# First weighted values in pairs, joined key and score pieces, and a bias from three bf16 terms

## Chip, cores, metric

One core of a Trainium2 chip. The time is the device time of one execution in microseconds (us). Times of whole kernels are from timed executions; points in time and lengths inside a kernel are from the one profiled execution of each, whose span is some 1.7 us shorter than its time. A halved clock is the granted clock of TensorE as the profile records it. Engines are called as in the profile: PE is TensorE, PEld its weight load, DVE is VectorE, ACT is ScalarE, POOL is GpSimd, SP is SyncE.

## The reference

Shapes: q, k, v are 4 x 8 x 768 x 64, `sort_net` is 4 x 8 x 8 x 8, `w_in` 512 x 2048, `w_out` 2048 x 512. All are f32.

```python
P = sort_net                                   # five rounds of row and column normalisation
for _ in range(5):
    P = P - np.max(P, axis=-1, keepdims=True)
    P = np.exp(P)
    P = P / (np.sum(P, axis=-1, keepdims=True) + 1e-09)
    P = P / (np.sum(P, axis=-2, keepdims=True) + 1e-09)
k_sorted = np.einsum('bhij,bhjcd->bhicd', P, k_b)      # blocks of 96 rows, mixed
v_sorted = np.einsum('bhij,bhjcd->bhicd', P, v_b)
scores = scale * np.matmul(q_b, k_sb.transpose(0, 1, 2, 4, 3))   # within a block
attn = softmax(scores)                                  # (written out in the reference)
x = (attn @ v_sb) as rows of 512                        # (3072 rows, heads side by side)
h = x @ w_in
r = np.maximum(h, 0.0)
g = s * (r * r) + b
out = g @ w_out
```

Since `g @ w_out` is s · (r² @ w_out) + b · (column sums of w_out), the kernel computes the second summand once, as a `bias` row that is the same for all rows.

## The kernel before

The 3072 rows go through in eight half-batches t = 0 to 7 of 384 rows. TensorE works through one long fixed order: the first layer `ffn1(t)` (the matmuls `hps`), the second layer `ffn2(t)` (the matmuls `ops`), and, between groups of four `ops`, small pieces of the attention of later half-batches. A `Queue` deals the pieces out, so many to a slot. Abbreviations in the queues: `S2` is two score pieces (`sc`), `P2` is two weighted-value pieces (`pv`), `K` is one key piece (`tk`), `V2` is one value piece (`tv`), `T` is the transposition of `x` by DMA and `q_turn` that of the queries.

The weighted values of one head pair, and the first ones of the kernel:

```python
def p_piece(t, hp, n0=0, nn=HB):
    ...
    for e in range(2):
        for n in range(n0, n0 + nn):
            nc.tensor.matmul(out=pv[e][...], lhsT=atf[:, c0:c0 + m],
                             rhs=VS[b][:, gi, :], start=True, stop=True)
    rec = rtp.tile([BLK, 2, HB], FP, tag="rec", name="rec")
    nc.vector.reciprocal(out=rec[:, :, 0:nn], in_=pvv[:, :, :, D])
    nc.vector.tensor_tensor(out=x[...], in0=pvv[:, :, :, 0:D], in1=rec[...], op=ALU.mult)
...
for hp in range(NHP):                    # the opening
    p_piece(0, hp, 0, 2)
    if hp == 3:
        t_part(0, 0, "s", 0, 2)
    warm_up(2, psa)
t_part(0, 2, "v", 0, 2)
warm_up(2, psa)
```

The column sums, made on GpSimd after a gate that holds them back until VectorE has written the last of half-batch 1, and the bias on TensorE:

```python
nc.gpsimd.tensor_copy(out=gate, in_=X[1][0:1, HB - 1, d_model - 1:d_model])
... # csum = wo_at(0) + wo_at(1), then csum += wo_at(f), f = 2 to 15, all on GpSimd, f32

def bias_piece():
    bps = psa.tile([128, 2, 512], FP, tag="a", name="bps")
    nc.tensor.matmul(out=bps[:, 0], lhsT=onesf, rhs=csum, start=True, stop=True)
    nc.vector.tensor_scalar(out=bias, in0=bps[:, 0], scalar1=b_bc, scalar2=None, op0=ALU.mult)
    ready.append(True)
    flush()                              # the rows that waited for the bias
```

The queue with the bias, and what follows it on GpSimd, where the loads from memory are issued:

```python
qu = Queue([nothing, lambda: q_piece(1, 2, "v")]
           + [lambda c0=c0: k_piece(1, c0, 16, 1, "vsv"[c0 // 32])() for c0 in range(0, BLK, 32)]
           + [seq(lambda: load_q(2), lambda: load_k(*brows(2)), bias_piece), V2[0], S2(2, 0), V2[1], S2(2, 2), V2[2], V2[3],
              P2(2, 0), V2[4], P2(2, 2), V2[5], S2(3, 0),
              seq(T(2), K(2, 0, 16, "s")), P2(3, 0), S2(3, 2), K(2, 32, 16, "s"), P2(3, 2), T(3),
              seq(lambda: q_turn(2), K(2, 64, 16, "s"))], 24)
ffn2(0, qu)
ffn2(1, qu)
ffn1(2)
ffn1(3)
nc.gpsimd.tensor_copy(out=gate2, in_=QT[2][0:1, NHP - 1, S - 1:S])   # waits for q_turn(2)
v_read(2, nc.gpsimd)                     # the weighted-value blocks vs of batch 2
load_k(*brows(3))
```

The softmax here doesn't subtract the row's maximum and nothing guards it: scores larger than these inputs give would overflow.

Of the kernel before, what the change touches and what calls it, by code (L numbers as in the profile page):

```python
# [18 lines left out]
def kernel(  # L19
# [74 lines left out]
    def load_k(rows, prow, n=1):  # L94
        for c0 in range(0, BLK, BLK // n):
            cs = slice(c0, c0 + BLK // n)
            nc.gpsimd.dma_start(out=kb[prow, cs, :], in_=kraw[rows, cs, :])
# [16 lines left out]
    VS = {}  # L114
# [37 lines left out]
    for c0 in range(0, d_ff, FCH):  # L152
# [1 line left out]
        nc.gpsimd.dma_start(  # L154
            out=w, in_=moe_w_in.rearrange("(hp p) f -> p hp f", p=128)[:, :, c0:c0 + FCH])
        wis.append(w)
    onesf = const.tile([128, 128], FP)
    nc.gpsimd.memset(onesf, 1.0)

    load_v(*brows(1))  # L160
    for f0 in range(0, NF, FW):
# [17 lines left out]
    def warm_up(n, pool=psb):  # L179
        wp = pool.tile([128, 256], FP, tag="b" if pool is psb else "a", name="wp")  # L180
        for _ in range(n):
            nc.tensor.matmul(out=wp, lhsT=zt[:, 0:128], rhs=zt, start=True, stop=True)  # L182
# [198 lines left out]
    def p_piece(t, hp, n0=0, nn=HB):  # L381

        b, half = divmod(t, 2)
        at = AT[t, hp]
        if t not in X:
            X[t] = xp.tile([BLK, HB, d_model], BF, tag="x", name="x")
        x = X[t]
        atf = at.rearrange("p e t -> p (e t)")
        if nn < HB:
            p1 = psb.tile([128, 512], FP, tag="b", name="pv")  # L390
            pv = [p1[:, e * nn * VW:(e + 1) * nn * VW] for e in range(2)]
            pvv = p1[0:BLK, 0:2 * nn * VW].rearrange("p (e n w) -> p e n w", e=2, w=VW)
        else:
            p2 = psa.tile([128, 2, 512], FP, tag="a", name="pv")
            pv = [p2[:, 0], p2[:, 1]]
            pvv = p2[0:BLK, :, 0:nn * VW].rearrange("p e (n w) -> p e n w", w=VW)
        for e in range(2):
            for n in range(n0, n0 + nn):
                c0 = (e * HB + n) * BLK
                m = 128 if c0 + 128 <= 2 * TG else BLK  # L400
                gi = e * 32 + hp * NB + half * HB + n
                nc.tensor.matmul(out=pv[e][0:m, (n - n0) * VW:(n - n0 + 1) * VW],  # L402
                                 lhsT=atf[:, c0:c0 + m],
# [3 lines that stand above are left out]
        nc.vector.tensor_tensor(  # L407
            out=x[:, n0:n0 + nn, hp * 128:(hp + 1) * 128].rearrange("p n (e d) -> p e n d", e=2),
            in0=pvv[:, :, :, 0:D],
            in1=rec[:, :, 0:nn].unsqueeze(3).broadcast_to([BLK, 2, nn, D]), op=ALU.mult)  # L410

    def t_piece(t, eng, n0=0, nn=HB):

        x = X[t]
        if t not in XT:
            XT[t] = xtp.tile([128, NHP, TG], BF, tag="xt", name="xt")
        if nn < HB:
            t1 = psb.tile([128, 1024], BF, tag="b", name="tr")
            tr = [t1[:, hp * nn * BLK:(hp + 1) * nn * BLK] for hp in range(NHP)]
            src = t1[:, 0:NHP * nn * BLK]  # L420
            dst = XT[t][:, :, n0 * BLK:(n0 + nn) * BLK]
            src = src.rearrange("p (a t) -> p a t", a=NHP)
        else:
            t2 = psa.tile([128, 2, 1024], BF, tag="a", name="tr")
            tr = [t2[:, hp // 2, (hp % 2) * TG:(hp % 2 + 1) * TG] for hp in range(NHP)]
            src = t2[:, :, 0:2 * TG]
            dst = XT[t].rearrange("p (a b) t -> p a (b t)", b=2)
        for hp in range(NHP):
            for n in range(n0, n0 + nn):
                nc.tensor.transpose(out=tr[hp][:, (n - n0) * BLK:(n - n0 + 1) * BLK],  # L430
                                    in_=x[:, n, hp * 128:(hp + 1) * 128],
                                    identity=ident[0:BLK, 0:BLK])
        evac(dst, src, eng)

    def t_part(t, hp0, eng, n0, nn):

        if t not in XT:
            XT[t] = xtp.tile([128, NHP, TG], BF, tag="xt", name="xt")
        tr = psa.tile([128, 2, 1024], BF, tag="a", name="tr")
        for i in range(2):  # L440
            hp = hp0 + i
            for n in range(n0, n0 + nn):
                nc.tensor.transpose(out=tr[:, 0, (i * nn + n - n0) * BLK:(i * nn + n - n0 + 1) * BLK],
                                    in_=X[t][:, n, hp * 128:(hp + 1) * 128],
                                    identity=ident[0:BLK, 0:BLK])
        evac(XT[t][:, hp0:hp0 + 2, n0 * BLK:(n0 + nn) * BLK],
             tr[:, 0, 0:2 * nn * BLK].rearrange("p (a t) -> p a t", a=2), eng)
# [13 lines left out]
    def nothing():  # L461
        pass

    def ffn1(t, slot=nothing, n0=0, nn=HB):
        if t not in GT:
            GT[t] = gtp.tile([128, NF, TG], BF, tag="gt", name="gt")
        gt = GT[t]
        c0, nt = n0 * BLK, nn * BLK
        for f0 in range(0, NF, 2):
            hps = psa.tile([128, 2, 512], FP, tag="a", name="hps")  # L470
            for f in range(2):
                for hp in range(NHP):
                    nc.tensor.matmul(out=hps[:, f, 0:nt], lhsT=wi_at(hp, f0 + f),  # L473
                                     rhs=xt_at(t, hp, n0, nn),
                                     start=(hp == 0), stop=(hp == NHP - 1))
            rt = rtp.tile([128, 2, TG], BF, tag="rt", name="rt")
            nc.scalar.activation(out=rt[:, :, 0:nt], in_=hps[:, :, 0:nt], func=AF.Relu)  # L477
            nc.vector.tensor_tensor(out=gt[:, f0:f0 + 2, c0:c0 + nt], in0=rt[:, :, 0:nt],  # L478
                                    in1=rt[:, :, 0:nt], op=ALU.mult)
            slot()  # L480
# [59 lines left out]
    def seq(*fs):  # L540
        def run():
            for f in fs:
                f()
        return run

    def S2(t, hp):
        return lambda: (s_piece(t, hp), s_piece(t, hp + 1))
# [9 lines left out]

    def bias_piece():
        bps = psa.tile([128, 2, 512], FP, tag="a", name="bps")
        nc.tensor.matmul(out=bps[:, 0], lhsT=onesf, rhs=csum, start=True, stop=True)  # L560
        nc.vector.tensor_scalar(out=bias, in0=bps[:, 0], scalar1=b_bc, scalar2=None,
                                op0=ALU.mult)
        ready.append(True)
        flush()
# [33 lines left out]
    v_piece0(56, 8, "v")  # L598
    s_piece(0, 2)
    s_piece(0, 3)  # L600
    for hp in range(NHP):
        p_piece(0, hp, 0, 2)
        if hp == 3:
            t_part(0, 0, "s", 0, 2)
        warm_up(2, psa)
    t_part(0, 2, "v", 0, 2)
    warm_up(2, psa)

    load_v(*brows(2))

# [1 line left out]
    def P(t, hp, *r):  # L612
        return lambda: p_piece(t, hp, *r)

    def SC(t, hp):
        return lambda: s_piece(t, hp)

    def V1(i, eng="s"):
        return lambda: v_piece1(i * 8, eng)

    ffn1(0, Queue([P(0, 0, 2, 2), P(0, 1, 2, 2), P(0, 2, 2, 2), P(0, 3, 2, 2),
                   lambda: q_half(1, "s"), lambda: t_piece(0, "v", 2, 2), SC(1, 0), SC(1, 1)], 8), 0, 2)
    ffn1(0, Queue([seq(SC(1, 2), P(1, 0)), V1(0), seq(SC(1, 3), P(1, 1)), V1(1), P(1, 2), P(1, 3),
                   seq(V1(2), V1(3)), lambda: t_piece(1, "v")], 8), 2, 2)
    V1(4)()
    V1(5)()
# [17 lines left out]
    load_v(*brows(3))  # L644
    csums(8, NF)

    def K(b, c0, nc2, eng):
        return lambda: k_piece(b, c0, nc2, 1, eng)()

    V2 = [lambda c0=c0: v_piece2(c0, "s") for c0 in range(0, BLK, 16)]  # L650
    qu = Queue([nothing, lambda: q_piece(1, 2, "v")]
               + [lambda c0=c0: k_piece(1, c0, 16, 1, "vsv"[c0 // 32])() for c0 in range(0, BLK, 32)]
               + [seq(lambda: load_q(2), lambda: load_k(*brows(2)), bias_piece), V2[0], S2(2, 0), V2[1], S2(2, 2), V2[2], V2[3],
                  P2(2, 0), V2[4], P2(2, 2), V2[5], S2(3, 0),
                  seq(T(2), K(2, 0, 16, "s")), P2(3, 0), S2(3, 2), K(2, 32, 16, "s"), P2(3, 2), T(3),
                  seq(lambda: q_turn(2), K(2, 64, 16, "s"))], 24)
    ffn2(0, qu)
    ffn2(1, qu)

# [6 lines left out]
    v_read(3, nc.gpsimd)  # L666
    load_q(3)
    qu = Queue([S2(4, 0), nothing, nothing, P2(4, 0), nothing, S2(4, 2), nothing, nothing,
                P2(4, 2), nothing, T(4), K(3, 0, 16, "v"), S2(5, 0), nothing, K(3, 32, 16, "s"),
                P2(5, 0), nothing, S2(5, 2), nothing, P2(5, 2), K(3, 64, 16, "s"), T(5),  # L670
                lambda: q_turn(3), nothing], 24)
    ffn2(2, qu)
    ffn2(3, qu)
# [39 lines left out]
```

## Time and profile before

| | before |
|---|---|
| time, median of 3 (range) | 233.44 us (233.39 to 233.68) |
| span of the profiled run | 231.6 us |
| PE busy | 224.3 us, 97% of the span |
| DVE, ACT, POOL busy | 50%, 49%, 21% |

The prediction below shows the main lines and reads them. TensorE is the bound: it hardly waits after the opening. One row of the view of what TensorE waits for says how little there is to win by removing waits (columns: engine and tile, what it waited for, us in total, times, longest):

```profile
PE ops L516 <- DVE ot L490: 0.4, 1, 0.4
```

This is the wait after the bias. After the start-up, up to 27 us, the view has only one more of note, 0.3 us for a Relu in the opening.

### The profile page before, as it was taken

The numbers are of one execution on the slowest core, as the hardware profiler recorded it, in microseconds if no ns is written. First come the engines' busy times: TensorE is split into PE (matmuls) and PEld (weight loads), VectorE is DVE, ScalarE is ACT, GpSimd is POOL, SyncE is SP. The second block draws the span as 40 slices with busy tenths as digits, with TensorE's granted clock in tenths as the row PEclk, the third lists the DMA queues.
The fourth block names the chain that finished last, engine by engine and source line by source line (L and its number), as shares of the span: only waits on it lengthen the run. The fifth ranks groups of instructions, "written<-read, shape, count | busy, mean of one in ns | idle before, by whom it ended". The sixth has DMA issues, their size and how long they took to land.

```text
span 231.6 us, 4837 instructions
## 1 busy us (share of the span) xinstructions
PE 224.3 (97%) x2036; PEld 136.8 (59%) x2036; DVE 116.8 (50%) x245; ACT 114.6 (49%) x164; POOL 48.3 (21%) x62
## 2 busy tenths in 40 slices
PE   8879999999999999999999999999999999999994
PEld 6779887765544555566555555665555556554442
DVE  5778566638992645244446653343452634432221
ACT  6168479685158486856630645656222236660000
POOL 7820000399992000007920000000000000000000
PEclk9975699999999999999999999999999999999999
DMA  5999999998799992764999995610115240001212
GB/s 93 142 200 211 226 193 205 231 220 183 106 110 180 273 312 63 161 82 65 130 148 133 183 197 115 93 47 0 46 47 113 93 110 4 3 0 45 80 59 91
DMA packets 46695, 28.90 MB, mean 125 GB/s; under 512 B 35921, under 2 KB 41041, under 8 KB 46161
## 3 DMA queue, kind: packets, MB, share of 16 engines
q0 software_dynamic: 18800, 15.21, 47.8%
q1 hardware_dynamic: 27728, 13.32, 26.6%
q8 instruction: 16, 0.26, 0.5%
q10 hardware_dynamic: 144, 0.07, 0.1%
q14 instruction: 7, 0.05, 0.1%
HBM read 29.63 MB, written 8.65 MB: 165 GB/s over the span
## 4 chain that ended last, share of the span: by engine, by line
PE 82%; DVE 7%; DMA 5%; ACT 3%; issue 1%; POOL 0%; POOLq 0%
PE hps L473 35%; PE ops L516 31%; DMA qr<-in_q_dram 5%; PE pv L402 4%; PE sc L375 3%; DVE gt L478 2%; ACT ks L240 2%; DVE ks L238 2%; PE tv L320 2%; PE ops L501 2%; PE tk L294 1%; PE tv L350 1%; PE wp L182 1%; PE tq L254 1%; PE tv L336 1%
## 5 line engine op out<-in xcount | busy, mean ns | idle before, releaser
L473 PE MATMUL hps<-xt,wi 128*128 128x384 bf16 (+1 forms) x576 | 87.1, 309 | 0.3 <-ACT rt L477 0.3
L516 PE MATMUL ops<-wo,gt 128*128 128x512 bf16 x368 | 86.9, 380 | 0.4 <-DVE ot L490 0.4
L473 PEld LDWEIGHTS <-wi 128*128 128x128 bf16 x576 | 54.1, 98 | 30.6 <-issue 1.3
L477 ACT ACTIVATE rt<-hps 128x768 bf16<-128x768 f32 (+1 forms) x72 | 53.1, 741 | 37.4 <-PE hps L473 37.0
L478 DVE TENSOR_TENSOR gt<-rt 128x768 bf16<-128x768 bf16 (+1 forms) x72 | 41.2, 574 | 50.2 <-ACT rt L477 50.0
L516 PEld LDWEIGHTS <-gt 128*128 128x128 bf16 x368 | 33.6, 98 | 37.2 <-issue 1.0
L378 ACT ACTIVATE at<-sc 96x768 bf16<-96x768 f32 x32 | 24.4, 804 | 27.7 <-PE sc L375 27.7
L490 DVE SCALAR_TENSOR_TENSOR ot<-ops,s_bc,bias 128x512 f32<-128x512 f32 x23 | 17.1, 749 | 41.2 <-PE ops L516 41.2
L240 ACT CAST ks<-tk 64x512 bf16<-64x512 f32 (+1 forms) x32 | 18.6, 582 | 10.5 <-PE tk L294 10.2
L407 DVE TENSOR_TENSOR x<-pv,rec 96x512 bf16<-96x512 f32 (+1 forms) x36 | 22.6, 627 | 1.3
L639 POOL TENSOR_TENSOR csum<-csum,wo 128x512 f32<-128x512 f32 x14 | 17.6, 1254 | 1.0
L402 PEld LDWEIGHTS <-at 96*128 96x128 bf16 (+1 forms) x256 | 12.0, 104 | 3.8
L182 PE MATMUL wp<-zt 128*128 128x256 bf16 x86 | 12.9, 311 | 1.1 <-DVE warm L113 1.1
L238 DVE CAST ks<-tk 64x512 bf16<-64x512 f32 (+1 forms) x20 | 13.0, 651 | 1.1 <-PE tk L294 0.8
L402 PE MATMUL pv<-vs,at 96*128 96x66 bf16 (+1 forms) x256 | 13.0, 199 | 0.1
L240 ACT CAST vn<-tv 128x512 bf16<-128x512 f32 (+1 forms) x12 | 9.4, 799 | 7.2 <-PE tv L350 5.0
L375 PEld LDWEIGHTS <-ks 64*96 64x96 bf16 x256 | 8.6, 128 | 5.8 <-issue 5.1
L406 DVE RECIPROCAL rec<-pv 96x8 f32<-96x8 f32 (+1 forms) x36 | 6.9, 192 | 9.5 <-PE pv L402 9.4
L84 POOL DMA_DIRECT2D qr<-in_q_dram x12 | 10.6, 912 | 4.8 <-DMA kb<-in_k_dram 3.1
L375 PE MATMUL sc<-qt,ks 64*96 64x96 bf16 x256 | 10.9, 219 | 0.1
L182 PEld LDWEIGHTS <-zt 128*128 128x128 bf16 x86 | 9.0, 110 | 2.6 <-DVE warm L113 1.1
L294 PEld LDWEIGHTS <-kb 64*128 64x128 bf16 x192 | 6.7, 99 | 3.9 <-issue 3.4
(73 smaller groups left out, 98.4 us busy)
## 6 DMA issues: line engine op xcount, KB each, us to landing
out_dram<-ot SPq DMA_DIRECT2D x23, 256.0 KB, 2.4
kb<-in_k_dram POOLq DMA_DIRECT2D x4, 768.0 KB, 12.2
vb<-in_v_dram POOLq DMA_DIRECT2D x4, 768.0 KB, 19.0
wi<-in_moe_w_in_dram POOLq DMA_DIRECT2D x2, 1024.0 KB, 19.7
wo<-in_moe_w_out_dram POOLq DMA_DIRECT2D x2, 1024.0 KB, 32.6
qr<-in_q_dram POOLq DMA_DIRECT2D x12, 128.0 KB, 13.5
dv<-vn SPq DMA_DIRECT2D x6, 256.0 KB, 7.5
vs<-dv POOLq DMA_DIRECT2D x4, 384.0 KB, 12.7
```

What stands on the lines that cost most here:

```text
L182: nc.tensor.matmul(out=wp, lhsT=zt[:, 0:128], rhs=zt, start=True, stop=True)
L238: nc.vector.tensor_copy(out=out, in_=in_)
L240: nc.scalar.copy(out=out, in_=in_)
L375: nc.tensor.matmul(out=sc[:, e, n * BLK:(n + 1) * BLK], lhsT=ks[pr, g0 + n, :], rhs=QT[b][pr, hp, q0:q0 + BLK], start=True, stop=True)
L378: nc.scalar.activation(out=at, in_=sc[:, :, 0:TG], func=AF.Exp, scale=scale)
L402: nc.tensor.matmul(out=pv[e][0:m, (n - n0) * VW:(n - n0 + 1) * VW], lhsT=atf[:, c0:c0 + m], rhs=VS[b][:, gi, :], start=True, stop=True)
L407: nc.vector.tensor_tensor(out=x[:, n0:n0 + nn, hp * 128:(hp + 1) * 128].rearrange("p n (e d) -> p e n d", e=2), in0=pvv[:, :, :, 0:D], in1 ...
L473: nc.tensor.matmul(out=hps[:, f, 0:nt], lhsT=wi_at(hp, f0 + f), rhs=xt_at(t, hp, n0, nn), start=(hp == 0), stop=(hp == NHP - 1))
L477: nc.scalar.activation(out=rt[:, :, 0:nt], in_=hps[:, :, 0:nt], func=AF.Relu)
L478: nc.vector.tensor_tensor(out=gt[:, f0:f0 + 2, c0:c0 + nt], in0=rt[:, :, 0:nt], in1=rt[:, :, 0:nt], op=ALU.mult)
L516: nc.tensor.matmul(out=ops, lhsT=gt[:, f, m * 128:(m + 1) * 128], rhs=wo_at(f), start=(f == 0), stop=(f == NF - 1))
L639: nc.gpsimd.tensor_tensor(out=csum, in0=csum, in1=wo_at(f), op=ALU.add)
```

## The change

Its intent is to take time out of TensorE's order in three ways: a quicker opening, fewer switches between full-height and 64-row matmuls (in the trace of before, four `ops` take 0.97 us after 64-row scores and 0.86 after a full-height product), and a bias without f32 matmuls.

Opening: weighted values of two head pairs at once, and a first layer that begins its first two `hps` tiles on the first two head pairs.

```diff
+    def p_pair(t, hp0, n0):             # two head pairs: 8 matmuls, one reciprocal, one multiply
+        ...
+        p2 = psa.tile([128, 4, 256], FP, tag="a", name="pv")
+        ...
-    for hp in range(NHP):
-        p_piece(0, hp, 0, 2)
-        if hp == 3:
-            t_part(0, 0, "s", 0, 2)
-        warm_up(2, psa)
+    warm_up(2)
+    p_pair(0, 0, 0)
+    warm_up(4)
+    p_pair(0, 2, 0)
+    t_part(0, 0, "s", 0, 2)
+    warm_up(3)
     t_part(0, 2, "v", 0, 2)
-    warm_up(2, psa)
...
-    def ffn1(t, slot=nothing, n0=0, nn=HB):
+    def ffn1(t, slot=nothing, n0=0, nn=HB, lead=0):
+        for f0 in range(0, lead, 2):    # lead = 4 in the first call only
+            begun[f0] = psa.tile([128, 2, 512], FP, tag="a", name="hps")
+            products(f0, begun[f0], range(0, NHP // 2))
...
-    ... seq(SC(1, 3), P(1, 1)), V1(1), P(1, 2), P(1, 3), ...
+    ... seq(SC(1, 3), P(1, 1)), P(1, 2), V1(1), P(1, 3), ...
```

Bias: the f32 column sums are split into three bf16 terms on GpSimd, and three bf16 matmuls add them up.

```diff
+    cparts = const.tile([128, 3, d_model], BF)
+    for i in range(3):
+        nc.gpsimd.tensor_copy(out=cparts[:, i], in_=csum)
+        if i < 2:
+            nc.gpsimd.tensor_tensor(out=csum, in0=csum, in1=cparts[:, i], op=ALU.subtract)
...
-        nc.tensor.matmul(out=bps[:, 0], lhsT=onesf, rhs=csum, start=True, stop=True)
+        for i in range(3):
+            nc.tensor.matmul(out=bps[:, 0], lhsT=ones, rhs=cparts[:, i], start=(i == 0),
+                             stop=(i == 2))
```

Joined pieces: key and score pieces share slots, one query copy goes to ScalarE, and `P2(3, 2)` comes one slot later.

```diff
-    qu = Queue([nothing, lambda: q_piece(1, 2, "v")]
-               + [... three key pieces of batch 1, one to a slot ...]
-               + [seq(lambda: load_q(2), lambda: load_k(*brows(2)), bias_piece), V2[0], ..., V2[5], S2(3, 0),
-                  seq(T(2), K(2, 0, 16, "s")), P2(3, 0), S2(3, 2), K(2, 32, 16, "s"), P2(3, 2), T(3),
-                  seq(lambda: q_turn(2), K(2, 64, 16, "s"))], 24)
+    qu = Queue([nothing, seq(lambda: q_piece(1, 2, "s"), K(1, 0, 16, "v")), nothing,
+                seq(K(1, 32, 16, "s"), K(1, 64, 16, "v")), nothing,
+                seq(lambda: load_q(2), lambda: load_k(*brows(2)), bias_piece),
+                V2[0], ..., V2[5],
+                seq(T(2), S2(3, 0), K(2, 0, 16, "v")), nothing, P2(3, 0), nothing,
+                seq(S2(3, 2), K(2, 32, 16, "s")), nothing, P2(3, 2),
+                seq(T(3), lambda: q_turn(2), K(2, 64, 16, "s"))], 24)
... the same for batch 3: S2(5, 0) with K(3, 0), S2(5, 2) with K(3, 32)
```

More of the change, by code (lines that the diff above doesn't have):

```diff
@@ L156 @@
         wis.append(w)
-    onesf = const.tile([128, 128], FP)
-    nc.gpsimd.memset(onesf, 1.0)
+    ones = const.tile([128, 128], BF)
+    nc.gpsimd.memset(ones, 1.0)
     load_v(*brows(1))
@@ L410, in p_piece @@
             in1=rec[:, :, 0:nn].unsqueeze(3).broadcast_to([BLK, 2, nn, D]), op=ALU.mult)
+    def p_pair(t, hp0, n0):
+        b, half = divmod(t, 2)
+        if t not in X:
+            X[t] = xp.tile([BLK, HB, d_model], BF, tag="x", name="x")
+        p2 = psa.tile([128, 4, 256], FP, tag="a", name="pv")
+        for i in range(2):
+            atf = AT[t, hp0 + i].rearrange("p e t -> p (e t)")
+            for e in range(2):
+                for n in range(2):
+                    c0 = (e * HB + n0 + n) * BLK
+                    gi = e * 32 + (hp0 + i) * NB + half * HB + n0 + n
+                    nc.tensor.matmul(out=p2[:, 2 * i + e, n * VW:(n + 1) * VW],
+                                     lhsT=atf[:, c0:c0 + 128], rhs=VS[b][:, gi, :],
+                                     start=True, stop=True)
+        pvv = p2[0:BLK, :, 0:2 * VW].rearrange("p a (n w) -> p a n w", w=VW)
+        rec = rtp.tile([BLK, 4, 2], FP, tag="rec", name="rec2")
+        nc.vector.reciprocal(out=rec, in_=pvv[:, :, :, D])
+        nc.vector.tensor_tensor(
+            out=X[t][:, n0:n0 + 2, hp0 * 128:(hp0 + 2) * 128].rearrange(
+                "p n (a d) -> p a n d", d=D),
+            in0=pvv[:, :, :, 0:D], in1=rec.unsqueeze(3).broadcast_to([BLK, 4, 2, D]),
+            op=ALU.mult)
     def t_piece(t, eng, n0=0, nn=HB):
@@ L468, in ffn1, with products @@
         c0, nt = n0 * BLK, nn * BLK
-        for f0 in range(0, NF, 2):
-            hps = psa.tile([128, 2, 512], FP, tag="a", name="hps")
+        begun = {}
+        def products(f0, hps, part):
             for f in range(2):
-                for hp in range(NHP):
+                for hp in part:
                     nc.tensor.matmul(out=hps[:, f, 0:nt], lhsT=wi_at(hp, f0 + f),
@@ L475, in ffn1 @@
                                      start=(hp == 0), stop=(hp == NHP - 1))
+        for f0 in range(0, lead, 2):
+            begun[f0] = psa.tile([128, 2, 512], FP, tag="a", name="hps")
+            products(f0, begun[f0], range(0, NHP // 2))
+        for f0 in range(0, NF, 2):
+            if f0 in begun:
+                hps = begun[f0]
+                products(f0, hps, range(NHP // 2, NHP))
+            else:
+                hps = psa.tile([128, 2, 512], FP, tag="a", name="hps")
+                products(f0, hps, range(NHP))
             rt = rtp.tile([128, 2, TG], BF, tag="rt", name="rt")
@@ L600 @@
     s_piece(0, 3)
-    for hp in range(NHP):
-        p_piece(0, hp, 0, 2)
-        if hp == 3:
-            t_part(0, 0, "s", 0, 2)
-        warm_up(2, psa)
+    warm_up(2)
[4 more added lines that the diff above has]
+    warm_up(3)
     t_part(0, 2, "v", 0, 2)
-    warm_up(2, psa)
     load_v(*brows(2))
@@ L621 @@
     ffn1(0, Queue([P(0, 0, 2, 2), P(0, 1, 2, 2), P(0, 2, 2, 2), P(0, 3, 2, 2),
-                   lambda: q_half(1, "s"), lambda: t_piece(0, "v", 2, 2), SC(1, 0), SC(1, 1)], 8), 0, 2)
-    ffn1(0, Queue([seq(SC(1, 2), P(1, 0)), V1(0), seq(SC(1, 3), P(1, 1)), V1(1), P(1, 2), P(1, 3),
+                   lambda: q_half(1, "s"), lambda: t_piece(0, "v", 2, 2), SC(1, 0), SC(1, 1)], 8), 0, 2, 4)
+    ffn1(0, Queue([seq(SC(1, 2), P(1, 0)), V1(0), seq(SC(1, 3), P(1, 1)), P(1, 2), V1(1), P(1, 3),
                    seq(V1(2), V1(3)), lambda: t_piece(1, "v")], 8), 2, 2)
@@ L650 @@
     V2 = [lambda c0=c0: v_piece2(c0, "s") for c0 in range(0, BLK, 16)]
-    qu = Queue([nothing, lambda: q_piece(1, 2, "v")]
-               + [lambda c0=c0: k_piece(1, c0, 16, 1, "vsv"[c0 // 32])() for c0 in range(0, BLK, 32)]
-               + [seq(lambda: load_q(2), lambda: load_k(*brows(2)), bias_piece), V2[0], S2(2, 0), V2[1], S2(2, 2), V2[2], V2[3],
-                  P2(2, 0), V2[4], P2(2, 2), V2[5], S2(3, 0),
-                  seq(T(2), K(2, 0, 16, "s")), P2(3, 0), S2(3, 2), K(2, 32, 16, "s"), P2(3, 2), T(3),
-                  seq(lambda: q_turn(2), K(2, 64, 16, "s"))], 24)
+    qu = Queue([nothing, seq(lambda: q_piece(1, 2, "s"), K(1, 0, 16, "v")), nothing,
+                seq(K(1, 32, 16, "s"), K(1, 64, 16, "v")), nothing,
+                seq(lambda: load_q(2), lambda: load_k(*brows(2)), bias_piece),
+                V2[0], S2(2, 0), V2[1], S2(2, 2), V2[2], V2[3], P2(2, 0), V2[4], P2(2, 2), V2[5],
+                seq(T(2), S2(3, 0), K(2, 0, 16, "v")), nothing, P2(3, 0), nothing,
+                seq(S2(3, 2), K(2, 32, 16, "s")), nothing, P2(3, 2),
+                seq(T(3), lambda: q_turn(2), K(2, 64, 16, "s"))], 24)
     ffn2(0, qu)
@@ L668 @@
     qu = Queue([S2(4, 0), nothing, nothing, P2(4, 0), nothing, S2(4, 2), nothing, nothing,
-                P2(4, 2), nothing, T(4), K(3, 0, 16, "v"), S2(5, 0), nothing, K(3, 32, 16, "s"),
-                P2(5, 0), nothing, S2(5, 2), nothing, P2(5, 2), K(3, 64, 16, "s"), T(5),
+                P2(4, 2), nothing, T(4), nothing, seq(S2(5, 0), K(3, 0, 16, "v")), nothing, nothing,
+                P2(5, 0), nothing, seq(S2(5, 2), K(3, 32, 16, "s")), nothing, P2(5, 2),
+                K(3, 64, 16, "s"), T(5),
                 lambda: q_turn(3), nothing], 24)
```

## The prediction

> **What bounds the kernel now.** I read the page first (busy slices, clock row, shares of the chain), then the chain in order of time, then the timeline at the three places that the diff touches, and last the engine that the diff gives new work, GpSimd (POOL).
>
> ```profile
> PE   8879999999999999999999999999999999999994
> PEclk9975699999999999999999999999999999999999
> PE 82%; DVE 7%; DMA 5%; ACT 3%; issue 1%; POOL 0%; POOLq 0%
> ```
>
> After the fifth slice (about 29 us) TensorE is busy in at least 90% of every slice but the last, and at full clock. The clock is low only from about 14 to 28 us. What shortens the kernel is therefore TensorE time taken out; what makes TensorE wait anywhere after 28 us is added to the end. The 7% of the chain on VectorE lie mostly between 54 and 70 us, where TensorE was nevertheless busy and VectorE's backlog ends in one wait of 0.41 us at 70.32.
>
> The opening, from the timeline and from the table of stretches (columns: stretch, length, busy time of PE, PEld, DVE, ACT, POOL, clock, DMA share, GB/s):
>
> ```profile
> 26.90 0.63 PE L182 MATMUL wp<-zt 128*128 128x256 bf16 x2
> 27.14 0.36 DVE L238 COPY xt<-tr 128x384 bf16<-128x384 bf16 x1 [0.43 <-PE tr L443]
> 27.32 1.05 PE L473 MATMUL hps<-xt,wi 128*128 128x192 bf16 x8
> ...
> 27.00:28.00 1.00, 1.00 (x10) 0.86 (x8) 0.36 (x1) 0.00 (x0) 0.00 (x0) 0.62 1.07 221
> ```
>
> The first layer (hps) starts only after the second transposed pair is copied. A mean clock of 0.62 over 27 to 28 us, half before and full after, puts the release at 27.76 (0.5x + 1 - x = 0.62, x = 0.76).
>
> The slots where weighted sums interleave with the second layer, from the chain in order of time (start, length, what):
>
> ```profile
> 80.78 0.43 PE tv L350 x2
> 81.21 0.86 PE ops L516 x4
> 82.08 0.49 PE sc L375 x16
> 82.56 0.97 PE ops L516 x4
> 83.53 0.58 PE tk L294 x16
> ```
>
> The same four ops matmuls take 0.86 after another full-height product but 0.97 after the 64-row scores (sc). The keys (tk) behave alike.
>
> The bias, from the timelines of POOL and of TensorE, and the wait that follows it:
>
> ```profile
> 44.73 1.14 POOL L637 TENSOR_TENSOR csum<-wo 128x512 f32<-128x512 bf16 x1
> 45.95 7.91 POOL L639 TENSOR_TENSOR csum<-csum,wo 128x512 f32<-128x512 f32 x6
> 53.81 0.54 POOL L100 DMA_DIRECT2D vb<-in_v_dram  x1
> 54.37 10.59 POOL L639 TENSOR_TENSOR csum<-csum,wo 128x512 f32<-128x512 f32 x8
> 64.90 5.31 POOL L84 DMA_DIRECT2D qr<-in_q_dram  x6
> 70.15 0.59 POOL L97 DMA_DIRECT2D kb<-in_k_dram  x1
> ```
>
> ```profile
> 66.06 1.03 PE L560 MATMUL bps<-csum,onesf 128*128 128x512 f32 x2
> 66.93 1.03 PE L516 MATMUL ops<-wo,gt 128*128 128x512 bf16 x4
> ...
> 70.32 1.02 PE L516 MATMUL ops<-wo,gt 128*128 128x512 bf16 x4 [0.41 <-DVE ot L490]
> ```
>
> This is the fact on which the prediction turns: POOL ends the column sums at 64.96 and TensorE uses them at 66.06, only 1.1 us later. POOL looks idle on the page (21%), but in this stretch it is full and almost on the critical path.
>
> [...] the trace has 1.14 to 1.36, median 1.26. [...] the drop at 14.12 (clock 0.56 over 14 to 15 us) and the release at 27.76 are 13.64 us apart[...].
>
> **The change part by part.**
>
> *Opening.* Four weighted-value pieces of one head pair become two of two. On VectorE that is 2 x (0.20 + 0.69) = 1.78 us in place of 4 x (0.18 + 0.42) = 2.40 (rows of rec and x, 512 and 256 elements). But the second pair now needs the fourth exponential, which ScalarE ends at 24.83. From there: eight products 0.5, rec and x 0.95, transposes 0.35, so the last transposes end near 27.0. The first-layer matmuls on the first two head pairs need not await the second copy and start at about 27.0, against 27.52 in the chain. The clock is still half until about 27.76, so the 0.5 us hold three matmuls of 160 ns, worth 82 ns each later: gain about 0.3 us.
>
> *Order of the later pieces.* One weighted-value piece is put before a value piece. In before, the two pieces at 41.3 and 42.25 fill the accumulators, and the chain shows 0.57 us (42.42 to 42.99) in which TensorE waits for the Relu. I take 0.35 us of it back.
>
> *Joined pieces.* Two key pieces share a slot once, and score and key pieces share one four times: five joins. A separate 64-row piece costs 0.11 on the way out and, from the starts in the timeline (ops end at 72.47, scores start at 72.57), some 0.1 on the way in, of which part is hidden; I take 0.15 each. One join lies before the bias, four after: 0.15 and 0.60 us.
>
> *One copy moved.* A query copy of 1.75 us goes from VectorE to ScalarE, which was idle for 4.79 us there. This removes the 0.41 us wait after the bias.
>
> *Bias.* On TensorE three bf16 matmuls of 512 columns (0.216 each, from ops: 0.86 for four) replace an f32 matmul in two passes that took 0.87: 0.65, a gain of 0.22 if all is ready. On POOL five operations come after the column sums: three copies to bf16 and two subtractions. Subtractions: 2 x 1.26 = 2.52. A copy of 512 is not in the trace; from POOL's memsets (0.21 for 128 elements, 0.30 for 256)[...], my estimate is 0.65, so 1.95. With the gaps of 0.07 between POOL operations: 4.8 us. The compiled order confirms that the three terms' matmuls wait for one copy each, and that these five stand before the six query loads and the key load.
>
> TensorE would reach the bias 0.3 + 0.35 + 0.15 = 0.8 us earlier, at 65.25. The sums start when the last weighted value of the second half is written, so they shift by 0.65: end 64.3, the third term at 69.1, the third matmul's end at 69.4. Before, the bias ended at 66.93. TensorE is 2.5 us behind there, although it has 0.8 us less to do. All later work waits in TensorE's order, so it counts in full.
>
> Sum on the path: +2.5 at the bias, -0.4 for the wait that goes, -0.6 for the four later joins = +1.5 us.
>
> **Two things that may be added.** The wait is about 4 us (65.25 to 69.4), broken by two short matmuls. [...] And the query and key loads of the third batch leave POOL some 4.2 us later: the key load is issued at about 74.4. It took 12.3 us before, much of it behind the query loads, and landed near 82.5 to 83; the key piece, now one slot earlier, wants it near 84. If it still takes 12.3 us, TensorE waits some 2 us; if the shorter queue lets it land in 7 to 9, nothing. +0.4 on average. The two overlap: a TensorE slowed by its clock waits less for the keys.
>
> **The rivals.** (1) The gains go through: POOL's five operations fit into the slack. Then 0.8 + 0.2 + 0.4 + 0.6 = 2 us less, 231.4. For it: the page's POOL share of 21%, and that whoever made the change can be supposed to have wanted this. Against it: 1.1 us of slack, plus 0.43 for two matmuls, against 4.8 us of work; even copies of 0.3 us make 3.7. (2) The wait is there, the clock falls and the keys are late too: +4.5 to +5.5, 238 to 239. [...] (3) The wait is there but shorter, 2 us, and the other gains cancel it: 233.5 to 234.5. For it: copies might be quicker than I estimate.
>
> **Range and chances.** The sum with the means of the two additions is +2.8, or 236.2; rival 1 and 3 pull it down, and I put the value at 235.6 us. The range is 232.3 to 238.4. Over 2% faster is below 228.8 us: no part can give 4.6 us, chance 0.01. Over 2% slower is above 238.1 us: it needs both additions nearly in full, 0.12. Within 2%: 0.87.
>
> **What would show it.** In the profile after: POOL's row with three copies near 0.65 and two subtractions near 1.26 from about 64.3 to 69.1; TensorE waiting on POOL at the bias matmuls by 3 to 4 us in all; no wait of the ops on ot just after; a clock below 1 in the slice after 69 us[...]; perhaps a wait of the first key piece on its load; the hps starting near 27.0; score and key pieces back to back with one 0.97 after them. The prediction is wrong if POOL's terms are ready within 2 us of the sums, or if TensorE comes to the bias much later than 65 us.

One term of its sum: +0.9 us for a halved clock at the bias (1.3 to 1.7 us with a chance of 0.6), of which length and chance were the author's estimate. With that term the sum came to 1.5 + 0.9 + 0.4 = +2.8 us, and the half clock is in the second rival's 4.5 to 5.5 too. The "1.14 to 1.36, median 1.26" are GpSimd's two-input operations of 512 elements in the trace of before. For a copy of 512, a line through the two memsets gives 0.48 us; the rest up to 0.65 was the author's estimate and not shown.

## The result

The changed kernel took 237.75 us (median of 4 runs, 237.52 to 237.87), the kernel before 233.43 us (median of 4, 233.39 to 233.68). All were fast runs. The ratio is 1.0182, with a 95% interval of 1.0164 to 1.0199: slower by 1.8%, inside the predicted range and 2.15 us above the predicted value. Ratios here and below are the mean time of one kernel's fast runs over that of the other's in the same rounds, so they are not quite the ratio of the medians. Executions over 1.5% slower than the fastest of the same kernel are left out of the means.

The page of the changed kernel, its busy slices, clock row and chain shares:

```profile
PE   8979999999949999999979999999999999999994
PEclk9975899999997999999999999999999999999999
PE 56%; issue 17%; POOL 13%; DVE 5%; DMA 5%; ACT 3%; POOLq 0%
```

Where before had nines there is now a 4 in the 12th slice (65 to 71 us), a clock of 7 in the slice behind it, and a 7 in the 21st (118 to 124 us). POOL, which had 0% of the chain that ended last, has 13%.

The timeline of POOL at the bias (start, length, line, operation):

```profile
64.87 0.61 POOL L687 CAST cparts<-csum 128x512 bf16<-128x512 f32 x1
65.56 1.15 POOL L689 TENSOR_TENSOR csum<-csum,cparts 128x512 f32<-128x512 f32 x1
66.78 0.61 POOL L687 CAST cparts<-csum 128x512 bf16<-128x512 f32 x1
67.46 1.15 POOL L689 TENSOR_TENSOR csum<-csum,cparts 128x512 f32<-128x512 f32 x1
68.68 0.61 POOL L687 CAST cparts<-csum 128x512 bf16<-128x512 f32 x1
...
74.48 0.60 POOL L97 DMA_DIRECT2D kb<-in_k_dram  x1
```

The five operations lie end to end from 64.87 to 69.29: 4.4 us. Only then do the loads follow, so the key load is issued at 74.48 instead of 70.15.

The timeline of TensorE at the same place; the bracket gives the idle time before, and what ended it:

```profile
65.53 0.38 PE L597 MATMUL bps<-cparts,ones 128*128 128x512 bf16 x1
67.44 0.38 PE L597 MATMUL bps<-cparts,ones 128*128 128x512 bf16 x1 [1.53 <-POOL cparts L687]
69.34 0.38 PE L597 MATMUL bps<-cparts,ones 128*128 128x512 bf16 x1 [1.53 <-POOL cparts L687]
69.56 0.68 PE L552 MATMUL ops<-wo,gt 128*128 128x512 bf16 x2
```

TensorE comes to the bias at 65.53, finds the first term just finished, and then twice waits 1.53 us. The `ops` after the bias start at 69.56; before, at 66.93. That is 2.63 us late, although TensorE had arrived 0.53 us earlier.

The table of stretches over the same time (columns: stretch, length, busy of PE, PEld, DVE, ACT, POOL, then the mean granted clock):

```profile
69.00:70.00 1.00, 0.66 (x3) 0.29 (x3) 0.24 (x1) 0.00 (x0) 1.00 (x2) 0.97 0.14 12
70.00:71.00 1.00, 0.78 (x3) 0.41 (x3) 0.96 (x2) 0.00 (x0) 1.00 (x2) 0.50 0.04 3
...
73.00:74.00 1.00, 1.00 (x19) 0.46 (x18) 0.40 (x1) 0.09 (x1) 1.00 (x2) 0.83 1.34 267
```

A mean of 0.97 puts the halving 0.06 us before 70, at 69.94; a mean of 0.83 puts the release 0.34 us after 73, at 73.34. So the clock was half for 3.40 us.

The third place is at 122 us, in the view of the changed kernel's waits:

```profile
PE bps L597 <- POOL cparts L687: 3.1, 2, 1.5
PE pv L402 <- DMA vs<-dv: 1.2, 1, 1.2
```

The first row is the bias again. The second was nowhere in the prediction: weighted values of batch 2 wait for `vs`, their blocks of v. The way to it starts with the transposition of `x` of half-batch 3, whose query transposes come behind it on the same queue and open the gate for the loads of `vs`. From the timelines of SP's queue and of TensorE, before:

```profile
91.74 1.28 SPq L452 DMA_TRANSPOSE xt<-x  x1
...
117.24 0.70 PE L402 MATMUL pv<-vs,at 96*128 96x66 bf16 x16
```

and after:

```profile
97.11 1.49 SPq L476 DMA_TRANSPOSE xt<-x  x1
...
122.07 0.69 PE L402 MATMUL pv<-vs,at 96*128 96x66 bf16 x16 [1.22 <-DMA vs<-dv]
```

Before, TensorE began the first layer of half-batch 2 at 92.38, 0.64 us after that transposition; after, at 95.83, 1.28 us ahead of it. The transposition has slipped by 1.9 us against TensorE. In both kernels the loads of `vs` are issued some 14 us after it (105.82 and 110.95).

How late TensorE is against before, place by place, shows where the time went:

| place | before | after | late by |
|---|---|---|---|
| second layer of half-batch 0 starts | 57.96 | 57.74 | -0.22 |
| bias | 66.06 | 65.53 | -0.53 |
| first `ops` after the bias | 66.93 | 69.56 | 2.63 |
| `ops` after the second score piece | 70.32 | 73.98 | 3.66 |
| first layer of half-batch 2 starts | 92.38 | 95.83 | 3.45 |
| weighted values of half-batch 4 | 117.24 | 122.07 | 4.83 |
| span | 231.6 | 236.0 | 4.4 |

From the third row to the fourth 1.03 us are lost. The half clock took more than that, since TensorE no longer waits for VectorE there: the same code takes 2.73 us from the one place to the other at full clock (69.97 to 72.70 in the filler run below) and 4.42 us here, so about 1.7 us. From the fourth to the fifth the joins give back 0.21, from the fifth to the sixth the new wait makes up 1.22 of 1.38 us, and after it the last two joins bring the lag from 4.83 down to 4.4.

The opening went earlier at its start and not at its end. From the timeline of TensorE after:

```profile
26.84 0.34 PE L467 MATMUL tr<-ident,x 96*128 96x96 bf16 x4 [0.51 <-DVE x L430]
27.02 1.16 PE L498 MATMUL hps<-xt,wi 128*128 128x192 bf16 x12
...
29.70 0.31 PE L402 MATMUL pv<-vs,at 96*128 96x66 bf16 x4 [0.25 <-DVE x L407]
```

The `hps` start at 27.02 as predicted (27.32 before). But since two of them are begun together, the first is complete later in the order, and its Relu starts on ScalarE only 0.19 us earlier (28.21 against 28.40). VectorE's work behind that Relu ends with the multiply `x` at 29.64, and at 29.70 TensorE has waited 0.25 us for it. At the query transposes that follow, it is still 0.19 us ahead (31.41 against 31.60), in a run whose clock happened to be released at 25.56 instead of 27.76.

### The profile page after: what moved, and what is told of

Same layout as the page of the kernel before. It is cut to its first block, busy times and chain, and to the rows that moved or that the text cites. A ratio compares the mean times of both kernels' runs of the same rounds, so it can differ in the third digit from the quotient of the medians.

```text
span 236.0 us, 4818 instructions
## 1 busy us (share of the span) xinstructions
PE 222.7 (94%) x2016; PEld 136.0 (58%) x2036; DVE 118.1 (50%) x244; ACT 113.5 (48%) x161; POOL 52.4 (22%) x67
## 4 chain that ended last, share of the span: by engine, by line
PE 56%; issue 17%; POOL 13%; DVE 5%; DMA 5%; ACT 3%; POOLq 0%
PE ops L552 23%; PE hps L498 21%; POOL csum L677 7%; DMA vs<-dv 4%; PE sc L375 3%; PE pv L402 2%; POOL qr L84 2%; PE tv L320 2%; PE ops L537 1%; ACT ks L240 1%; POOL csum L689 1%; POOL cparts L687 1%; DVE x L407 1%; PE tq L254 1%; DMA sn<-in_sort_net_dram 1%
## 5 line engine op out<-in xcount | busy, mean ns | idle before, releaser
L552 PE MATMUL ops<-wo,gt 128*128 128x512 bf16 x348 | 84.0, 383 | 1.5 <-issue 0.5
L514 DVE TENSOR_TENSOR gt<-rt 128x768 bf16<-128x768 bf16 (+1 forms) x72 | 41.7, 581 | 49.0 <-ACT rt L513 48.8
L552 PEld LDWEIGHTS <-gt 128*128 128x128 bf16 x368 | 34.3, 99 | 39.9 <-issue 3.1
L407 DVE TENSOR_TENSOR x<-pv,rec 96x512 bf16<-96x512 f32 (+1 forms) x32 | 20.9, 654 | 1.2
L240 ACT CAST ks<-tk 64x512 bf16<-64x512 f32 (+1 forms) x28 | 16.3, 582 | 3.6 <-PE tk L294 3.3
L238 DVE CAST ks<-tk 64x512 bf16<-64x512 f32 (+1 forms) x24 | 15.8, 658 | 3.1 <-PE tk L294 2.7
L240 ACT CAST vn<-tv 128x512 bf16<-128x512 f32 (+1 forms) x12 | 9.4, 800 | 10.5 <-PE tv L350 9.8
L182 PE MATMUL wp<-zt 128*128 128x256 bf16 x85 | 12.5, 314 | 1.1 <-DVE warm L113 1.1
L402 PEld LDWEIGHTS <-at 96*128 96x128 bf16 x240 | 10.5, 102 | 4.9 <-issue 1.7
L402 PE MATMUL pv<-vs,at 96*128 96x66 bf16 x240 | 11.3, 195 | 1.5 <-DMA vs<-dv 1.2
L84 POOL DMA_DIRECT2D qr<-in_q_dram x12 | 10.6, 912 | 4.7 <-DMA kb<-in_k_dram 2.9
L406 DVE RECIPROCAL rec<-pv 96x8 f32<-96x8 f32 (+1 forms) x32 | 6.2, 195 | 6.7 <-PE pv L402 6.7
L240 ACT COPY qt<-tq 128x768 bf16<-128x768 bf16 (+1 forms) x6 | 5.9, 1014 | 5.0 <-PE tq L254 3.3
```

Of the source, the lines that this page charges most:

```text
L182: nc.tensor.matmul(out=wp, lhsT=zt[:, 0:128], rhs=zt, start=True, stop=True)
L240: nc.scalar.copy(out=out, in_=in_)
L402: nc.tensor.matmul(out=pv[e][0:m, (n - n0) * VW:(n - n0 + 1) * VW], lhsT=atf[:, c0:c0 + m], rhs=VS[b][:, gi, :], start=True, stop=True)
L407: nc.vector.tensor_tensor(out=x[:, n0:n0 + nn, hp * 128:(hp + 1) * 128].rearrange("p n (e d) -> p e n d", e=2), in0=pvv[:, :, :, 0:D], in1 ...
L514: nc.vector.tensor_tensor(out=gt[:, f0:f0 + 2, c0:c0 + nt], in0=rt[:, :, 0:nt], in1=rt[:, :, 0:nt], op=ALU.mult)
L552: nc.tensor.matmul(out=ops, lhsT=gt[:, f, m * 128:(m + 1) * 128], rhs=wo_at(f), start=(f == 0), stop=(f == NF - 1))
```

## The experiments

Theory: the terms on GpSimd are the loss (2.6 us of lateness and the half clock), the later `P2(3, 2)` causes the wait for `vs`, and opening and joins gain a little. Rival 1: the joins lose by themselves, since they ask for keys sooner. Rival 2: the lost time is half clock, and a busy TensorE would get it back. Three batches ran on three chips; the kernel before had medians of 233.25, 233.36 and 233.24 us there. Every kernel gave correct results. Ratios are against before.

| kernel | time, fast runs (us) | ratio, 95% interval |
|---|---|---|
| changed, bias in f32 | 233.54 to 235.62 (3) | 1.0054, 0.9997 to 1.0112 |
| before, with the three terms | 235.72 to 238.44 (4) | 1.0167, 1.0120 to 1.0214 |
| changed, filler between the terms | 236.38 to 237.66 (4) | 1.0161, 1.0131 to 1.0192 |
| changed, `P2(3, 2)` and `T(3)` as before | 236.59 to 238.32 (4) | 1.0184, 1.0151 to 1.0218 |
| before, with the opening | 233.14 to 233.72 (5) | 1.0003, 0.9992 to 1.0015 |
| before, with the joins | 232.73 to 235.77 (6) | 1.0040, 1.0007 to 1.0073 |
| changed, f32 bias, loads early | 231.66 to 232.28 (5) | 0.9944, 0.9932 to 0.9955 |
| the same, terms begun early | 232.49 to 234.47 (6) | 1.0009, 0.9987 to 1.0031 |
| before, joins, loads early | 231.74 to 232.36 (5) | 0.9946, 0.9934 to 0.9959 |
| changed, loads early | 234.73 to 236.08 (4) | 1.0097, 1.0074 to 1.0119 |
| the same, filler | 234.73 to 235.35 (5) | 1.0074, 1.0062 to 1.0086 |

### The bias back to f32

```diff
-        for i in range(3):
-            nc.tensor.matmul(out=bps[:, 0], lhsT=ones, rhs=cparts[:, i], ...)
+        nc.tensor.matmul(out=bps[:, 0], lhsT=onesf, rhs=csum, start=True, stop=True)
```

(and no `cparts` on GpSimd)

> The changed kernel with the bias taken back to one f32 matmul on the f32 column sums, all else kept. Theory (the three terms on GpSimd make TensorE wait, and that wait halves the clock): the 3.1 us of waiting on the terms, the stretch at half clock and nearly all of the loss go; 232.5 to 233.5 us, clock 1.00 over 66 to 76 us. Rival (the opening or the regrouped slots cost time themselves): it stays above 235 us.

Three fast runs of 233.54, 234.34 and 235.62 us (a fourth of 239.16 is slow and not used). So most of the loss goes, but the gain over before that the theory wanted is not there. The view of waits names why, with 0.6 us for `vs` besides:

```profile
PE tk L294 <- DMA kb<-in_k_dram: 1.1, 1, 1.1
```

Without the wait at the bias, TensorE reaches the first joined key piece before its load has landed (issued at 70.71, it took 12.5 us). The changed kernel did not show this, because it was late itself.

### The three terms alone

The bias part of the change, applied to the kernel before.

> The kernel before with only the bias changed to three bf16 terms. Theory: TensorE comes to the bias at 66.1 us, the third term is there at about 69.4; +2.7 us of lateness, +1.3 for the half clock, -0.4 for the VectorE wait that is hidden: 236.6 to 237.5 us. Rival (the loss needs the regrouped slots, which bring TensorE to the bias earlier): below 235 us.

As expected: 1.0167, some 3.9 us. The profile shows 2.7 us of wait on `cparts`, and half clock from 69.38 to 72.8. The four runs follow their mean granted clock: 235.72 us at 0.978, 237.29 and 237.40 at 0.964, 238.44 at 0.955. This kernel alone would nearly explain the whole loss.

### Filler between the terms

```diff
         for i in range(3):
+            for _ in range(10 if i else 0):
+                nc.tensor.matmul(out=bps[:, 1, 0:256], lhsT=zt[:, 0:128], rhs=zt, start=True, stop=True)
             nc.tensor.matmul(out=bps[:, 0], lhsT=ones, rhs=cparts[:, i], ...)
```

Ten matmuls on zeros, into an unused half of the tile, keep TensorE busy while it would wait: 2.56 of the 3 us from 66 to 69, against 0.38 in the changed kernel.

> The changed kernel with ten filler matmuls of zeros (256 columns, into the unused second bank of the bias tile) in front of the second and of the third term's matmul. They fit into the wait (10 x 0.11 us against 1.5 us of idle time) and delay nothing. Theory: the clock stays at 1.00 after 69 us and the time falls by 1.3 us to about 236.4. Rival (the half clock costs nothing since later waits absorb it): 237.7 as the changed kernel.

The clock stayed at 1.00 after 69 us, and the wait on `cparts` fell to 0.9 us; yet the ratio fell only from 1.0182 to 1.0161, less than the theory said. The timeline of TensorE shows where the rest went:

```profile
86.36 0.64 PE L294 MATMUL tk<-pd,kb 64*128 64x64 bf16 x16 [1.40 <-ACT at L378]
...
121.97 0.69 PE L402 MATMUL pv<-vs,at 96*128 96x66 bf16 x16 [0.82 <-DVE ot L526]
```

The first wait is put down to ScalarE, whose `at` also ended just before it (86.33). But the weight load of the same piece is put down to the key load, which was issued at 74.89 and landed 11.4 us later, at 86.3; and in the changed kernel the piece starts (86.08) before that ScalarE operation does (86.10). The second is put down to VectorE (`ot` ended at 121.93), but the second load of `vs` landed at about the same time, and in the changed kernel it is this load that the same piece waits for. The changed kernel, at half clock, came to the same piece at 86.08 and did not wait. So the half clock and the wait for the keys stand for each other there, which also fits that its four runs, with mean clocks of 0.971 to 0.978, differ by only 0.35 us.

### `P2(3, 2)` in its old slot

The edit moves `T(3)`, the transposition that needs it, back along with it.

```diff
-                seq(S2(3, 2), K(2, 32, 16, "s")), nothing, P2(3, 2),
-                seq(T(3), lambda: q_turn(2), K(2, 64, 16, "s"))], 24)
+                seq(S2(3, 2), K(2, 32, 16, "s")), P2(3, 2), T(3),
+                seq(lambda: q_turn(2), K(2, 64, 16, "s"))], 24)
```

> The changed kernel with the last weighted-value pair of the third group one slot earlier, and the transpose that follows it in a slot of its own, as before; the score and key joins are kept. Theory: the later query transposes, the gate on them and the two loads of weighted blocks start 1 us sooner, so the wait of 1.22 us on these loads at 122 us falls to 0.0 to 0.4: 236.5 to 236.9 us. Rival (those loads are late because GpSimd is behind since the bias): 237.7 us, wait kept.

The wait is gone from the profile, and the timeline of SP's queue shows the transposition back in its place, 0.63 us ahead of the first layer of half-batch 2 (97.32):

```profile
96.69 1.28 SPq L476 DMA_TRANSPOSE xt<-x  x1
```

So in this kernel the later slot made the wait. The old slot does not always prevent one: two later runs that have it wait 0.7 us (terms begun earlier) and 0.5 us (changed kernel with early loads) at the same place, where the second of these loads took 10.6 and 10.2 us instead of 9.5 before. Why it took longer is not shown. The time did not fall, and for that this run is inconclusive: in the profiled execution two stretches of 3.41 us were at half clock (68.70 to 75.54), not one, and the two runs without that (mean clock 0.978) took 237.68 and 236.59 us. That the key load held these up is argued from the filler run, not shown.

### The opening alone

> The kernel before with the opening alone (pairs, first layer begun on two head pairs, the order of one later piece). The prediction gave it 0.65 us: 232.6 to 232.9. The traces so far speak against: with the clock released at the same moment (27.7 us) the changed kernel and its variants come to the bias only 0.0 to 0.1 us sooner than before. Theory now: nothing is gained, 233.0 to 233.5 us, and the runs spread by up to 1 us with the moment of the clock's release.

No gain at all: 1.0003, in a tight interval. The profile shows the same wait of 0.25 us for `x` (at 29.86) and the query transposes at 31.58 against 31.60 before. What the order of the later pieces wins (42.81 against 42.99) is gone at the bias, 66.00 against 66.06, and `ops` starts at 70.32 in both, released by VectorE in both.

### The joined pieces alone

> The kernel before with the regrouped slots alone (joined key and score pieces, one copy moved). Theory (the key piece, one slot earlier, waits for its load, and the weighted values of the next batch wait for theirs): a wait of 1.0 to 1.5 us on the key load near 83 us and about 0.6 on the other near 118, against 0.9 us saved: 233.6 to 234.6 us. Rival (the joins only save, as the prediction had it, 0.15 us each and the 0.4 us wait): 232.2 to 232.7 us.

Rival 1 is right: by themselves the joins cost 1.0040, about 0.9 us (0.2 to 1.7 by the interval). From the view of TensorE's waits, where `vs` adds 0.8 us:

```profile
PE tk L294 <- DMA kb<-in_k_dram: 1.2, 1, 1.2
```

The key load is issued at 70.84 (70.15 before) and takes 12.6 us; the key piece wants it at 82.3 instead of 83.5. Two new waits of 2.0 us in all cancel the matmul switches saved, the removed wait of 0.41 us, and more.

### f32 bias, and both loads early

The changed kernel with the f32 bias, `P2(3, 2)` in its old slot, and the key load issued ahead of the six query loads:

```diff
-                seq(lambda: load_q(2), lambda: load_k(*brows(2)), bias_piece),
+                seq(lambda: load_k(*brows(2)), lambda: load_q(2), bias_piece),
```

> The changed kernel with the f32 bias, the last weighted-value pair of the third group a slot earlier as in the run before, and the key load of the third batch issued ahead of its six query loads. Theory (what the regrouped slots save is eaten by two late loads): both waits are gone and the saving shows; 231.6 to 232.3 us, faster than both kernels. Rival (the saving isn't there, or another wait takes its place): 233.3 us or more.

232.03 us, 0.9944: faster than both kernels. Both waits are gone. From the timelines of POOL and of TensorE:

```profile
65.27 0.54 POOL L97 DMA_DIRECT2D kb<-in_k_dram  x1
```

```profile
81.75 0.63 PE L294 MATMUL tk<-pd,kb 64*128 64x64 bf16 x16
```

The load, 5 us earlier and no longer behind 768 KB of queries, takes 9.6 us and is there 6.9 us before its use.

### The terms begun earlier

The same with the three terms, and the GpSimd gate opened by an earlier value, so that the column sums begin at 38.6 us and the terms are ready at 64.5:

```diff
-    nc.gpsimd.tensor_copy(out=gate, in_=X[1][0:1, HB - 1, d_model - 1:d_model])
+    nc.gpsimd.tensor_copy(out=gate, in_=X[1][0:1, HB - 1, 127:128])
```

> The run before, but with the three bf16 terms as in the change and the column sums on GpSimd begun at the first instead of the last weighted value of the second group, some 5 to 6 us sooner. Theory (the terms cost only because they end too late): they are ready at about 64 us, TensorE doesn't wait at the bias, the clock stays up: 231.4 to 232.5 us. Rival (GpSimd's work in itself slows VectorE, or the terms are slow to use): above 233.5 us.

There is no wait at the bias, and yet 233.74 us (median), missing 231.4 to 232.5. The profile has two waits that the run before has not: 0.7 us for `vs` at 118 us, and one in the opening. From the timelines of VectorE and of TensorE:

```profile
38.62 2.60 DVE L514 TENSOR_TENSOR gt<-rt 128x384 bf16<-128x384 bf16 x2 [0.21 <-ACT rt L513]
```

```profile
42.12 0.83 PE L498 MATMUL hps<-xt,wi 128*128 128x192 bf16 x8 [1.26 <-DVE x L407]
```

This VectorE operation takes 0.36 us just before the sums begin (at 37.22), and 1.3 us each in this pair, beside the first two of GpSimd's sums (the first starts at 38.62 and takes 1.14 us; the pair starts at 38.62 and takes 2.60). In the run before, whose sums begin at 45.11, it takes 0.36 us each time at the same place (38.80 and 39.90). Not every overlap costs as much: beside later sums the same operation takes 0.36 to 0.66 us (43.51 to 46.90). GpSimd's operations are longer as well beside this VectorE operation: from 59.42 to 62.55, with `gt` from 58.27 to 62.09, two copies take 0.82 us and a subtraction 1.34, where the changed kernel has 0.61 and 1.15. Presumably the gate was there to keep the two apart; here the column sums could not be moved ahead for nothing.

### The kernel before with joins and early loads

> The kernel before with the regrouped slots, the weighted-value pair a slot earlier and the key load ahead of the query loads; bias in f32, opening as before. Theory (the opening gives nothing): 231.7 to 232.3 us, as the run with the new opening (232.03). Rival (the opening's 0.65 us of the prediction is hidden somewhere and shows once the loads are early): 232.6 us or more.

231.90 us, 0.9946: the same as with the opening (0.9944). It is the simplest of the fast versions, and leaves the opening no gain that these runs could resolve (each interval is 0.3 us to either side). With their loads in time the joins, together with the moved copy, gain about 1.3 us.

### The changed kernel with early loads, without and with filler

The two edits of the early loads applied to the changed kernel, then the filler as well.

> The changed kernel, three bf16 terms kept, with the weighted-value pair a slot earlier and the key load first. Neither load is waited for. Theory: what is left is the wait on the terms (3.1 us) and the half clock after it: 235.8 to 237.0 us, with a spread of over 1 us that goes with the mean clock. Rival (the late loads were the greater part): below 235 us.

> The run before with the ten filler matmuls ahead of the second and the third term. Theory (the half clock costs 1 to 1.5 us of its own; with the filler alone the late loads had eaten it): 234.8 to 235.4 us, that is 232.03 of the f32 version plus 3.05 us of waiting, and little spread. Rival (the half clock costs nothing): as the run before.

Without filler the fast runs lie at 234.73 to 236.08 us, all at a mean clock of 0.978 (two more at 0.955, 238.33 and 238.65 us, count as slow and are not used; 0.956 was the mean clock of the profile with two halved stretches, so 1.0097 may be this kernel's time without a half clock). Its profile has the same 3.1 us of wait on `cparts` as the changed kernel and 0.5 us for `vs`. With filler all five runs lie within 0.7 us, no load is waited for, and the view of waits has at the bias only:

```profile
PE bps L600 <- POOL cparts L690: 0.9, 2, 0.4
```

Here the clock is full and the loads are in time, so the terms stand alone: 1.0074 against 0.9944 is 0.0130, or 3.0 us of 233.4. That is the price of the splitting on GpSimd, before any half clock. The profile without filler has no halved stretch at the bias (clock 1.00 from 66 to 76 us), so what the filler gains over these fast runs, 0.0023 or 0.5 us, is about the wait for `vs` that it does not have. What the half clock costs once the loads are in time stays open.

## Why the prediction was right or wrong

- **GpSimd's slack and the wait at the bias: right.** The terms took 4.4 us where 4.8 was predicted (copies 0.61 us, estimated 0.65; subtractions 1.15, estimated 1.26). TensorE was 2.63 us late behind the bias, predicted 2.5. Its arrival, 65.53 in place of 65.25, is partly luck: with a later clock release the same code arrives at 66.0 (filler runs 65.94 and 66.02), no earlier than before. That 2.63 meets 2.5 is partly luck too: the terms took less than estimated but began at 64.87 and not at 64.3, since the gate of the column sums opened at 44.36, hardly before its 44.40 in the kernel before. Removing or adding the terms alone moves the time by 3.0 to 3.9 us.
- **The half clock: right in kind and, in the profile, in size.** Predicted as 1.3 to 1.7 us with a chance of 0.6 (an estimate that the trace of before did not show); the profile lost about 1.7. That it lengthens this kernel is not shown: two of its four runs had a mean clock of 0.977 and 0.978, the most that any profile without a halved stretch after the opening has, so they presumably had none; they took 237.75 and 237.87 us, no less than the other two. Its place has a measured regularity. The halved stretch lasts 3.40 us here (69.94 to 73.34), 3.42 with the terms alone (69.38 to 72.80), and 6.84, twice that, with `P2` in its old slot (68.70 to 75.54). The time from the clock's release in the opening to the halving is a whole number of such lengths in all three profiles: 44.38 us here (release at 25.56), or 13 x 3.414; 40.96 us with the terms alone (28.42) and with `P2` in its old slot (27.74), or 12 x 3.413. The wait alone does not decide whether it comes: the changed kernel with early loads waits the same 1.5 us twice at the bias, and its clock stays at 1.00. What decides it is not shown.
- **"The two overlap": right.** The changed kernel's key load took 10.5 us and was not waited for; half clock and late keys replaced each other, as the filler run showed.
- **The VectorE wait: right.** The 0.41 us after the bias are gone.
- **The opening, 0.3 + 0.35 us: wrong.** The step that failed is counting a start 0.3 us earlier as a gain that lasts. Two `hps` begun together bring the first Relu forward by 0.19 us only, and TensorE then waits 0.25 us for VectorE behind it. The 0.35 us were also more than there was to win: the 0.57 us of the chain from 42.42 to 42.99 are mostly the Relu's own 0.50, while the timeline has TensorE idle for 0.31; likewise the start at 27.52 that the 0.5 us were counted from is the chain's, and the timeline has 27.32. Alone the opening measured 1.0003. With the clock released at nearly the same moment (27.7 to 27.8 us), the second layer of half-batch 0 starts at 57.96 before and at 58.15 to 58.26 in three runs with the opening (both filler runs, and `P2` in its old slot).
- **The joined pieces, 0.15 us each: the term was mis-signed as a whole.** The switches do save that order of time, but the prediction looked for late keys only as a consequence of GpSimd's 4 us, and let a join cost nothing otherwise. In fact the key piece, a slot earlier, met its load without any delay on GpSimd: 1.2 us of wait. The joins cost 0.9 us alone, in place of a gain of 0.75 from the joins and 0.4 from the moved copy. With the loads in time they give 1.3 us, so the sum was about right there. The profile of the run with f32 bias and both loads early divides it: the join before the bias gives 0.31 us (7.79 us from the start of the second layer to the bias, 8.10 before), the VectorE backlog that the moved copy takes away 0.66 (`ops` after the second score piece at 69.66, 70.32 before), the next two joins 0.21 and the last two 0.36.
- **A wait that no step had: `vs` at 122 us.** Moving `P2(3, 2)` one slot later was read in the diff and not followed further. It delays a transposition, the query transposes behind it, the gate, and the loads: 1.2 us. Before, the `vs` loads had just made it; the joins alone, which include that move, wait 0.8 us for them.

Together: terms alone 3.9 us, joins alone 0.9, opening 0; the sum of 4.8 and the 4.25 measured differ by less than the intervals of the first two (1.2 and 0.8 us to either side). What is open is how much of the changed kernel's time in each single run is half clock and how much the wait for keys: only profiled runs show which.

## What to carry to other kernels

Ask of a helper engine when its result is ready, not how busy it is: GpSimd had 21% of the span and 1.1 us of slack. A piece that is moved forward or joined to another uses its load sooner, and one that is moved back delays what hangs on it; follow both to the next load before counting the gain. A wait can hide behind another one, so the cost of a part is seen only when the other waits are taken away.
